# Gate and up tiles beside the last chunk's attention: three filled groups a tile in place of two, with fewer plain steps ahead of them

## The chip, the core and the metric

The kernel runs on one core of a Trainium2 chip. The metric is the device time of one execution in microseconds; of several runs the median is given. A core has TensorE (matmuls; PE in the profile, its weight loads PEld), VectorE (DVE), ScalarE (ACT), GpSimd (POOL) and SyncE (SP, which here only issues transfers). Each engine works through its own queue in order. Matmuls write to PSUM, which has eight banks of 128 x 512 fp32 here, and the other engines read the results there.

## The reference

One transformer block on 2048 rows of width 512, with 32 heads of 16 and a gated feed-forward of width 1792; the six modulation vectors come from a condition `c`.

```python
h = _layernorm(x, axis=-1) * (1 + ca) + sa
x = x + ga * _A_ref(h, A_wqkv, A_wo)          # softmax attention, then wo
h = _layernorm(x, axis=-1) * (1 + cb) + sb
x = x + gb * _B_ref(h, B_w_gate, B_w_up, B_w_down)   # (silu(x@w_gate) * (x@w_up)) @ w_down
```

## The kernel before, in words

The rows are worked on in four chunks of 512 queries. After the projections the kernel is one long attention loop: 32 units (four chunks of eight groups of four heads), each of 16 **steps**, 512 steps in all; a step is one tile of 128 keys. While the attention of one chunk runs, the output projection and the feed-forward of the chunk before are done beside it. The stretch of this change lies beside the last chunk's attention, where the feed-forward of chunk 2 (the last but one, `ci == last - 1`) is done.

A step has four **pairs** (`pair_of`, L982). A pair is one score matmul (`score`, L565: keys by queries, 50 rows of the array, 512 columns) and one matmul for the row maxima of a unit 20 steps ahead (`max_one`, L514: 48 rows). The two use opposite halves of the array's rows and run side by side. ScalarE turns the score into an exponential (L573), VectorE reduces the other one (L525); until they have read their bank, no new matmul can write it. Which banks serve is set by `bank` for scores and `four` for maxima. For the last 20 steps no maxima are left, and a pair is a score alone.

The order of the work is written out by hand, in two forms:

- `plain(steps)` (L1046) issues windows of three pairs and then some PV steps (`pv_step`, L575: exponentials by values, all 128 rows). Scores use three banks (4, 5, 6), maxima four (0, 3, 1, 2). Two PV half steps belong to each attention step; at the end of a plain stretch one more is issued, to catch up.
- `filled(places, work)` (L1061) issues eight pairs, which is two steps, with other work between them, and then the PV half steps that are due (four, once it runs). After pair r it takes `places[r]` **slots** of the work. A slot is two matmuls on opposite row halves (L789), one into each of the two banks of `FBANKS`, 3 and 6. Scores have two banks (4, 5), maxima three (0, 1, 2), bank 7 gathers the PV sums. When the maxima are over, `ALONE` replaces the places, and scores take turns over five banks.

A **gate and up tile** (`gate_up`, L854) computes 128 of the 1792 columns, gate in one bank and up in the other: 24 slots, 12 in each of two phases (`accumulate`, L778). In the second phase the two row halves trade banks. The two phases fill two groups with the places `TWO`, twelve slots each, and the PV matmuls stand between them. At the last slot ScalarE is given `th` (the tanh of the gate, L862). The rest, `q` (L866) and `m` (L868) on VectorE and the split of `m` on POOL (L870, L871), is put on the list `posts`; `hook()` (L914) issues what is on the list, at the end of each group. The tile's call also issues the next tile's 1 MB weight load on SP (`load_gu`, L713). The **down** steps (`down`, L878) have twelve slots in one group, with the places `DOWN`; their row halves trade banks too, and there a wait on ScalarE (L798) stands between the phases: it waits for the first phase's last matmuls, and the second phase's first matmul waits for it.

What belongs to a step's number (loads of the next units, the closing of a unit, the turning of the row maxima) is issued by `after(i)` from `end_steps` (L1040) and stays with that number. The row maxima of a unit are turned by `max_rows` (L527) if this falls in a plain stretch, and by `max_turned` (L545), with eight small DMAs on SP, if it falls in a filled one.

For chunk 2 the loop at L1090 issues plain steps up to step 403, four groups for the output projection, twelve plain steps for the second layer norm, then `REST` = 24 plain steps, and then the jobs: tiles 0, 1 and 2, two down steps, two tiles, two down steps, and so on up to tile 10. The nine tiles 0 to 8 take 36 steps before the change. Tile 8 ends where the maxima do.

Of the kernel before, what the change touches and what calls it, by code (L numbers as in the profile page):

```python
# [45 lines left out]
PTS = 13  # L46
FBANKS = (3, 6)
KEEP = 7
REST = 24
NORM = 9  # L50
STARTS = (147, 275, 403)
TWO = (0, 3, 2, 2, 2, 2, 1, 0)
DOWN = (0, 3, 3, 0, 3, 3, 0, 0)
ALONE = {TWO: (0, 4, 0, 4, 0, 4, 0, 0), DOWN: (0, 6, 0, 0, 0, 6, 0, 0)}


def run(it):
    for _ in it:
        pass


def take(it, k):
    run(islice(it, k))
# [40 lines left out]
def block_kernel(ctx, tc, x, wqkv, wo, w_gate, w_up, w_down, c, w_mod, out):  # L104
# [393 lines left out]
    last = NC - 1  # L498
# [132 lines left out]
    def tile_mid():  # L631
        return pf.tile([P, 2, CW], F32R, name="mid", tag="mid", bufs=3)

    def tmp(name):
        return pf.tile([P, CW], F32, name=name, tag="tmp", bufs=4)
# [142 lines left out]
    def accumulate(outs, lhs, rhs, nk, after, halves, by_k=False, trade=False):  # L778
        ends = []


        terms = [(k, a, b) for k in range(nk) for a, b in ((0, 0), (0, 1), (1, 0))]
        z = len(terms) - 1
        if halves:
            for ph in range(2):
                for j, (k, a, b) in enumerate(terms):
                    for e in (ph, 1 - ph):
                        rows = slice(64 * (ph ^ e), 64 * (ph ^ e) + 64)
                        mm = nc.tensor.matmul(outs[e], lhs(e, a, k)[rows], rhs(b, k)[rows],  # L789
                                              start=(ph == 0 and j == 0), stop=(j == z and (ph == 1 or trade)),  # L790
                                              skip_group_check=(ph == 1 and trade))
                        if trade and j == z * (1 - ph):
                            if ph == 0:
                                ends.append(mm.ins.name)
                            else:
                                tc.add_manual_dep(mm.ins, seen.ins.name, SYNC, reason="row halves trade banks")
                    if trade and j == z and ph == 0:
                        seen = nc.scalar.nop()  # L798
                        for name in ends:
                            tc.add_manual_dep(seen.ins, name, SYNC, reason="row halves trade banks")  # L800
                    if j == z and ph:
                        after()
                    yield
        else:
            order = [(e, j) for e in range(2) for j in range(z + 1)]
            for e, j in sorted(order, key=lambda o: o[1] // 3) if by_k else order:
                k, a, b = terms[j]
                nc.tensor.matmul(outs[e], lhs(e, a, k), rhs(b, k), start=(j == 0), stop=(j == z))  # L808
                if e == 1 and j == z:
                    after()  # L810
                yield
# [31 lines left out]
    def out_pair(ch, t0, outs, halves):  # L843
        return accumulate(outs, lambda e, a, k: ch.oT[a][:, k, (t0 + e) * P:(t0 + e + 1) * P],
                          lambda b, k: ch.wo[k // 2][:, b, k % 2, :], NK,
                          lambda: posts.append(lambda: add_o(ch, t0, outs, True)), halves)
# [4 lines left out]
                nc.tensor.matmul(pt, ch.oT[a][:, k, t * P:(t + 1) * P], ch.wo[k // 2][:, b, k % 2, :],  # L851
                                 start=(k == 0 and a == b == 0), stop=(k == NK - 1 and a == 1))

    def gate_up(ch, f, outs, halves):  # L854
        ch.load_gu(f + ch.ahead)
        if f == 0:
            ch.load_wd(0)
        ch.mid[f] = mid = tile_mid()

        def after():  # L860
            th = tmp("th")
            nc.scalar.activation(th, outs[0], AF.Tanh, scale=0.5)  # L862

            def later():
                q = tmp("q")
                nc.vector.scalar_tensor_tensor(q, th, 1.0, outs[0], op0=ALU.add, op1=ALU.mult)  # L866
                m32 = tmp("m32")
                nc.vector.tensor_mul(m32, outs[1], q)  # L868
                slow = halves or (ch.ci, f) == (last - 1, NF - 2)
                (nc.gpsimd.tensor_copy if slow else nc.scalar.copy)(mid[:, 0, :], m32)  # L870
                (nc.gpsimd if slow else nc.vector).tensor_sub(mid[:, 1, :], m32, mid[:, 0, :].bitcast(F32))  # L871
            posts.append(later)

        w = ch.w.pop(f)
        return accumulate(outs, lambda e, a, k: w[:, 2 * e + a, k, :], lambda b, k: ch.hT[b][:, k, :], NK, after,
                          halves)

    def down(ch, m, t0, outs, halves):  # L878
        def later():
# [27 lines left out]
    def scaled(ch):  # L907
        ch.load_gu(0)
        ch.norm_scale(nc.gpsimd)
        ch.nt = [tile_mid().bitcast(F32) for _ in range(2)]  # L910
        for t in range(4):
            ch.normalize(t)

    def hook():  # L914
        while posts:
            posts.pop(0)()
# [61 lines left out]
    halves = [(i, half) for i in range(n) for half in range(2)]  # L978
# [3 lines left out]
    def pair_of():  # L982
        nonlocal done
        i = done // 4 - 1
        most = 4 * n - 4 * (LEAD - 1)
        h = (ORDER if done < most else (0, 1, 2, 3))[done % 4]
        work = [lambda: score(i + 1, h)]
        if done < most:
            work.insert(1 - h % 2, lambda: max_one(done + 4 * (LEAD - 1)))
        for f in work:  # L990
            f()
        done += 1
        if side:
            side.pop(0)()

    for i in range(-LEAD, -1):
# [7 lines left out]
        if i == -2:  # L1004
            four, work = three, bank
# [11 lines left out]
    def pvs(most, by_halves):  # L1017

        nonlocal owed
        if by_halves:  # L1020
            most, owed = most + owed, 0
        while most and halves and 4 * halves[0][0] + 8 <= done:
            i, half = halves.pop(0)
            pv_step(i, half)
            most -= 1
            if i % 16 == 15 and half:
                close_unit(i // 16, done // 4 - 1)
                if by_halves:
                    break
        if by_halves and most and halves and 4 * halves[0][0] + 8 <= done:  # L1030
            owed = most

    def turns_behind():
        for b in list(behind):
            b[0] -= 1
            if not b[0]:
                b[1]()
                behind.remove(b)

    def end_steps():  # L1040
        nonlocal ended
        while ended < done // 4:
            after(ended - 1)
            ended += 1

    def plain(steps, tails=()):  # L1046

        nonlocal four, bank, beside
        beside = False
        assert steps % WIN == 0 and done % 4 == 0  # L1050
        four, bank = Turn(0, 3, 1, 2), Turn(4, 5, 6)
        for w in range(4 * steps // WIN):
            for _ in range(WIN):
                pair_of()
            if w < len(tails) and tails[w]:
                tails[w](four())
            pvs((HALVES[(w - 2) % 4] if done > 8 else 0) + (w == 4 * steps // WIN - 1), True)
            turns_behind()
            end_steps()

    def filled(places, work):  # L1061

        nonlocal four, bank, beside
        beside = True
        four, bank = three, Turn(4, 5)
        if done >= 4 * n - 4 * (LEAD - 1):
            places, bank = ALONE.get(places, places), Turn(4, 5, 0, 1, 2)
        for r in range(len(places)):
            pair_of()
            take(work, places[r])  # L1070
            if r % 4 == 3:
                end_steps()
        hook()
        pvs(6, False)
        turns_behind()
# [12 lines left out]
    outs = [banks[b] for b in FBANKS]  # L1088
    pvs(3, False)
    for ci in range(last):  # L1090
        plain(STARTS[ci] - done // 4)
        ch = chunks[ci]
        for t0 in (0, 2):
            work = out_pair(ch, t0, outs, True)
            filled(TWO, work)
            filled(TWO, work)
        behind.append([4, lambda: scaled(ch)])
        tails = [lambda tp, k=k: ch.turned(tp, k) for k in range(NK)]
        plain(NORM, [None] * NORM + tails[:3])
        plain(WIN, tails[3:])  # L1100
        if ci == last - 1:
            plain(REST)
        for _ in range(len(ch.jobs) - (KEEP if ci == last - 1 else 0)):
            job, args = ch.jobs.pop(0)
            if args == (NF // FG - 1, 0):
                plain(WIN)
            work = job(ch, *args, outs, True)
            for places in (TWO, TWO) if job is gate_up else (DOWN,):
                filled(places, work)
    chunks[last - 1].load_gu(NF - 2)  # L1110
    filled((0,) * 4, iter(()))

# [22 lines left out]
    ch, chp = chunks[last], chunks[last - 1]  # L1135
# [54 lines left out]
```

## Time and profile before

| | us |
|---|---|
| median of 3 runs (lowest to highest) | 1827.27 (1826.89 to 1827.74) |
| the profiled execution's own time | 1826.86 |
| its span, first to last instruction | 1825.0 |

The profile is of one execution. The page's first part gives each engine's busy time; its fourth part follows the chain of work that ended last, back from the end. Windows cut the span into stretches, the view in order of time lists single instructions. A matmul's row starts when it starts; its end is modelled, so matmuls that follow each other overlap in the rows (0.39 us long, one every 0.23 us). "L571 PE" is the score's matmul, "L571 PEld" the load of its weights. An arrow behind an idle time names what ended it. Lines are those of the kernel before. In all views of one execution times count from the span's start.

### The profile page before, as it was taken

What the parts mean: (1) busy time and instruction counts of PE and PEld (TensorE: products, weight loads), DVE (VectorE), ACT (ScalarE), POOL (GpSimd) and SP (SyncE); (2) the same over time, 40 slices, a digit from 0 to 9 for tenths busy, and PEclk for the clock granted to TensorE, in tenths of its full rate; (3) what the DMA queues carried; (4) which work ended last, traced back from release to release, by engine and by line L of the source; (5) the groups of instructions that cost most, each with busy time, mean ns of one, the idle gap of its engine ahead of it and who ended that gap; (6) DMA issues with size and microseconds to landing.
All of it is one profiled execution on the core that took longest, in us unless ns stands there. A gap on an engine that the chain in (4) does not pass through costs nothing.

```text
span 1825.0 us, 40961 instructions
## 1 busy us (share of the span) xinstructions
PE 1816.3 (100%) x16904; PEld 1202.5 (66%) x16904; DVE 1521.2 (83%) x2554; ACT 1248.0 (68%) x2358; POOL 459.9 (25%) x538
## 2 busy tenths in 40 slices
PE   9999999999999999999999999999999999999999
PEld 7876444444465777776565777776564577777887
DVE  5578999999999888888999888889999988832544
ACT  4223888888888766777888767767888876673211
POOL 3612544556223111111123111111113011131200
PEclk9999999999999999999999999999999999999999
DMA  9883876667845444453544554444643536333742
GB/s 307 288 232 138 203 199 172 179 167 199 207 81 125 103 122 143 115 149 70 145 110 105 141 125 118 122 118 91 161 80 57 116 90 157 134 123 120 279 167 108
DMA packets 80486, 267.62 MB, mean 147 GB/s; under 512 B 19604, under 2 KB 24212, under 8 KB 59620
## 3 DMA queue, kind: packets, MB, share of 16 engines
q1 hardware_dynamic: 61324, 179.71, 34.0%
q0 software_dynamic: 18288, 84.49, 19.5%
q8 instruction: 133, 2.18, 0.5%
q10 hardware_dynamic: 688, 0.80, 0.1%
q14 instruction: 53, 0.43, 0.1%
HBM read 201.85 MB, written 62.13 MB: 145 GB/s over the span
## 4 chain that ended last, share of the span: by engine, by line
PE 83%; DVE 14%; ACT 1%; DMA 0%; issue 0%; SPq 0%; DVEq 0%
PE bank L586 21%; PE bank L789 20%; PE bank L571 14%; DVE mx L525 14%; PE bank L523 11%; PE bank L808 8%; PE bank L213 7%; PE bank L851 1%; PE bank L772 0%; DMA wm_ab<-in_w_mod 0%; PE bank L165 0%; ACT sq L832 0%; DVE v_flat L882 0%; PE bank L537 0%; SPq L261 0%
## 5 line engine op out<-in xcount | busy, mean ns | idle before, releaser
L525 DVE TENSOR_REDUCE mx<-bank 128x1 f32<-128x512 f32 x2048 | 1273.3, 681 | 111.0 <-PE bank L523 63.7
L571 PE MATMUL bank<-qop,kop 50*128 50x512 f32 x2048 | 729.7, 426 | 0.4 <-ACT pt__16494 L573 0.2
L523 PE MATMUL bank<-kop,qop 48*128 48x512 f32 x2048 | 724.6, 425 | 0.3
L571 PEld LDWEIGHTS bank<-qop,kop 50*128 50x128 f32 x2048 | 343.1, 184 | 168.9 <-issue 49.8
L523 PEld LDWEIGHTS bank<-kop,qop 48*128 48x128 f32 x2048 | 342.8, 184 | 106.2 <-DVE mx L525 62.1
L789 PE MATMUL bank<-act,wgu 64*128 64x512 f32 x1872 | 303.5, 392 | 0.0
L789 PEld LDWEIGHTS bank<-act,wgu 64*128 64x128 f32 x1872 | 199.4, 187 | 22.5
L613 POOL TENSOR_TENSOR on<-o,rb 128x512 f32<-128x512 f32 x31 | 39.9, 1286 | 507.8 <-DMA rb<-d_dr 359.0
L789 PE MATMUL bank<-wd,mid 64*128 64x512 f32 x912 | 131.6, 391 | 0.0
L870 POOL CAST mid<-m 128x512 fp32r<-128x512 f32 x40 | 24.4, 609 | 380.5 <-DVE m L868 273.7
L789 PEld LDWEIGHTS bank<-wd,mid 64*128 64x128 f32 x912 | 92.2, 186 | 11.2
L213 PE MATMUL bank<-hT,wqs 128*128 128x512 f32 x384 | 94.4, 397 | 0.4 <-DVE wqs L353 0.4
L866 DVE SCALAR_TENSOR_TENSOR q<-th,bank 128x512 f32<-128x512 f32 x56 | 38.3, 683 | 54.2 <-ACT th L862 54.2
L213 PEld LDWEIGHTS bank<-hT,wqs 128*128 128x128 f32 x384 | 70.6, 188 | 19.1 <-issue 3.2
L862 ACT ACTIVATE th<-bank 128x512 f32<-128x512 f32 x56 | 33.2, 594 | 57.9 <-PE bank L808 57.9
L882 DVE TENSOR_TENSOR x<-bank,x 128x512 f32<-128x512 f32 x84 | 53.9, 685 | 16.1 <-PE bank L789 16.1
L868 DVE TENSOR_TENSOR m<-bank,q 128x512 f32<-128x512 f32 x56 | 38.7, 692 | 21.7 <-PE bank L808 19.7
L871 POOL TENSOR_TENSOR mid<-m,mid 128x512 fp32r<-128x512 f32 x40 | 51.7, 1292 | 3.3
L808 PE MATMUL bank<-wd,mid 128*128 128x512 f32 x216 | 51.3, 393 | 0.0
L213 PE MATMUL bank<-wqs,hT 128*128 128x512 f32 x192 | 48.0, 398 | 0.0
L789 PE MATMUL bank<-wgu,act 64*128 64x512 f32 x288 | 47.6, 392 | 0.0
L808 PEld LDWEIGHTS bank<-wd,mid 128*128 128x128 f32 x216 | 40.4, 188 | 8.9
(6300 smaller groups left out, 5137.3 us busy)
## 6 DMA issues: line engine op xcount, KB each, us to landing
wgu<-gu_dr SPq DMA_DIRECT2D x48, 1024.0 KB
wd<-wd_dr SPq DMA_DIRECT2D x28, 1024.0 KB
kop<-kd SPq DMA_DIRECT2D x33, 768.0 KB
kop<-kd POOLq DMA_DIRECT2D x29, 768.0 KB, 8.8
gu_dr<-wgu POOLq DMA_DIRECT2D x14, 1024.0 KB, 13.6
kd<-prt SPq DMA_DIRECT2D x16, 512.0 KB
qd<-prt SPq DMA_DIRECT2D x16, 512.0 KB
kop<-gu_dr SPq DMA_DIRECT2D x8, 1024.0 KB
```

The costliest lines, as they stand in the source:

```text
L213: nc.tensor.matmul(pt, lhs(a, k), rhs(b, k), start=(n == 0), stop=(n == 3 * nk - 1))
L523: nc.tensor.matmul(pm, qop[u][rows, s, qt * P:(qt + 1) * P], kop[u % 3][rows, s, kc * CW:(kc + 1) * CW], start=True, stop=True)
L525: nc.vector.tensor_reduce(mx[u][:, b, s, qt, kc:kc + 1], pm, op=ALU.max, axis=AX.X)
L571: nc.tensor.matmul(sp, kop[u % 3][rows, h // 2, kt * P:(kt + 1) * P], qop[u][rows, h // 2, :], start=True, stop=True)
L586: nc.tensor.matmul(pv[u][32 * h:32 * h + 32, cols], v_flat[:, e0:e0 + 32], p_[h][:, cols], start=(kt == 0 and half == 0), stop=(kt == 15), ...
L613: mul.tensor_mul(on, o, rb)
L789: mm = nc.tensor.matmul(outs[e], lhs(e, a, k)[rows], rhs(b, k)[rows], start=(ph == 0 and j == 0), stop=(j == z and (ph == 1 or trade)), sk ...
L808: nc.tensor.matmul(outs[e], lhs(e, a, k), rhs(b, k), start=(j == 0), stop=(j == z))
L866: nc.vector.scalar_tensor_tensor(q, th, 1.0, outs[0], op0=ALU.add, op1=ALU.mult)
L868: nc.vector.tensor_mul(m32, outs[1], q)
L871: (nc.gpsimd if slow else nc.vector).tensor_sub(mid[:, 1, :], m32, mid[:, 0, :].bitcast(F32))
L882: nc.vector.tensor_add(ch.x2[:, t, :], outs[e], ch.x2[:, t, :])
```

## The change

Tiles 0 to 8 of chunk 2 (`SPREAD` = 9) are spread over three filled groups in place of two, with 9, 8 and 7 slots (`THREE`). Each tile thus takes six steps, two more than before, and `REST` falls from 24 plain steps to 6, so that the number of steps is the same. The first phase now ends inside the second group, after its first three slots; so these tiles get the wait of the down steps between their phases (`trade`). With `soon`, `hook()` is called after each pair too, so `q`, `m` and the split are issued right after the last slot's pair (pair 5 of the third group) and no longer at the group's end. The third group of tile 8 lies where no maxima are left and has places of its own in `ALONE`.

```diff
-REST = 24
+REST = 6
...
-ALONE = {TWO: (0, 4, 0, 4, 0, 4, 0, 0), DOWN: (0, 6, 0, 0, 0, 6, 0, 0)}
+THREE = ((0, 2, 2, 1, 2, 1, 1, 0), (0, 3, 0, 2, 1, 1, 1, 0), (0, 2, 2, 1, 1, 1, 0, 0))
+SPREAD = 9
+ALONE = {THREE[2]: (0, 4, 0, 3, 0, 0, 0, 0), TWO: (0, 4, 0, 4, 0, 4, 0, 0), DOWN: (0, 6, 0, 0, 0, 6, 0, 0)}
...
-    def gate_up(ch, f, outs, halves):
+    def gate_up(ch, f, outs, halves, trade=False):
...
         return accumulate(outs, lambda e, a, k: w[:, 2 * e + a, k, :], lambda b, k: ch.hT[b][:, k, :], NK, after,
-                          halves)
+                          halves, trade=trade)
...
-    def filled(places, work):
+    def filled(places, work, soon=False):
...
             take(work, places[r])
+            if soon:
+                hook()
             if r % 4 == 3:
                 end_steps()
...
-            work = job(ch, *args, outs, True)
-            for places in (TWO, TWO) if job is gate_up else (DOWN,):
-                filled(places, work)
+            spread = job is gate_up and ci == last - 1 and args[0] < SPREAD
+            work = job(ch, *args, outs, True, *((True,) if spread else ()))
+            for places in THREE if spread else (TWO, TWO) if job is gate_up else (DOWN,):
+                filled(places, work, spread)
```

## Rows read from the trace of the kernel before

**Rows 1.** The page: busy time by engine; the chain that ended last, by engine.

```profile
PE 1816.3 (100%) x16904; PEld 1202.5 (66%) x16904; DVE 1521.2 (83%) x2554; ACT 1248.0 (68%) x2358; POOL 459.9 (25%) x538
...
PE 83%; DVE 14%; ACT 1%; DMA 0%; issue 0%; SPq 0%; DVEq 0%
```

**Rows 2.** Windows, score matmuls alone (L571, PE): stretch, its us, busy (count), clock.

```profile
1393.47:1452.40 58.93, 33.11 (x96) 1.00 0.31 57
1408.02:1444.11 36.09, 20.42 (x60) 1.00 0.43 71
...
1506.80:1533.95 27.15, 12.56 (x32) 1.00 0.79 185
...
1601.76:1608.32 6.56, 3.26 (x8) 1.00 0.47 176
1608.32:1614.14 5.82, 1.70 (x9) 1.00 0.03 5
```

**Rows 3.** Windows, all engines: plain stretch, one tile; PE, PEld, DVE, ACT, POOL.

```profile
1393.47:1452.40 58.93, 58.80 (x592) 28.58 (x588) 58.22 (x101) 50.88 (x102) 4.91 (x6) 1.00 0.31 57
1466.07:1479.61 13.54, 13.54 (x148) 10.55 (x144) 11.66 (x19) 9.62 (x17) 1.91 (x2) 1.00 0.57 125
```

**Rows 4.** Groups by line, plain stretch 1408.02 to 1444.11: busy, mean ns | idle before.

```profile
L525 DVE TENSOR_REDUCE mx<-bank 128x1 f32<-128x512 f32 x62 | 37.2, 674 | 0.0
```

**Rows 5.** Order of time, one filled group with twelve slots: start, length, instruction.

```profile
1527.18 0.50 PE L571 MATMUL bank<-qop,kop 50*128 50x512 f32 x1
...
1527.52 0.39 PE L571 MATMUL bank<-qop,kop 50*128 50x512 f32 x1
...
1528.36 0.18 PEld L571 LDWEIGHTS bank<-qop,kop 50*128 50x128 f32 x1
...
1529.17 0.40 PE L571 MATMUL bank<-qop,kop 50*128 50x512 f32 x1
...
1529.88 0.39 PE L571 MATMUL bank<-qop,kop 50*128 50x512 f32 x1
...
1531.74 0.41 PE L571 MATMUL bank<-qop,kop 50*128 50x512 f32 x1
...
1533.95 0.49 PE L571 MATMUL bank<-qop,kop 50*128 50x512 f32 x1
```

**Rows 6.** Order of time, the same group: ScalarE and VectorE.

```profile
1527.71 0.60 ACT L573 ACTIVATE pt__18965<-bank 128x512 f32<-128x512 f32 x1 [1.67 <-PE bank L523]
1528.21 0.59 ACT L573 ACTIVATE pt__18970<-bank 128x512 f32<-128x512 f32 x1
...
1529.63 0.60 ACT L573 ACTIVATE pt__18992<-bank 128x512 f32<-128x512 f32 x1
1530.31 0.60 ACT L573 ACTIVATE pt__18999<-bank 128x512 f32<-128x512 f32 x1
...
1532.91 0.68 DVE L866 SCALAR_TENSOR_TENSOR q<-th,bank 128x512 f32<-128x512 f32 x1
1533.62 0.69 DVE L868 TENSOR_TENSOR m<-bank,q 128x512 f32<-128x512 f32 x1
```

**Rows 7.** Order of time, p2 of the group at 1513.56, after a late exponential.

```profile
1514.82 0.40 PE L523 MATMUL bank<-kop,qop 48*128 48x512 f32 x1
1514.83 0.18 PEld L571 LDWEIGHTS bank<-qop,kop 50*128 50x128 f32 x1
1514.83 0.49 PE L571 MATMUL bank<-qop,kop 50*128 50x512 f32 x1
```

**Rows 8.** Line L571, 1452.40 to 1608.32: idle before it until (us, times).

```profile
  ACT pt__19691 L573: 0.2, 1
```

**Rows 9.** Line L798, the wait between phases: count, ns min/median/max.

```profile
L798 ACTq EVENT_SEMAPHORE  x38: 17/17/17, 630.2 to 1656.6; - x38
```

**Rows 10.** Order of time, filled groups: SP and POOL.

```profile
1500.66 4.38 SPq L562 DMA_DIRECT2D qop<-turned  x8
...
1521.44 1.29 POOL L871 TENSOR_TENSOR mid<-m,mid 128x512 fp32r<-128x512 f32 x1
```

## The prediction

> **What bounds the kernel now.** I read the page first: TensorE counts as busy for the whole span, and the chain that ended last lies on it for 83% [rows 1]. Its busy time is modelled, so this alone does not say that it is full. Next I cut the stretch beside the last chunk's attention into windows and counted its score matmuls, four to a step [rows 2]. The 24 plain steps ahead of the tiles take 58.93 us; 15 of them, clear of both ends, take 36.09 us, or 2.406 us a step. Four filled groups of two steps, which are two gate and up tiles, take 27.15 us: 6.79 us a group, 13.58 us a tile. The two kinds have different limits. In the plain stretch VectorE is busy for 58.22 of 58.93 us [rows 3], and its maxima follow each other with no idle time [rows 4], 60 of them in the 36.09 us, 0.60 us each. In a filled tile VectorE has work for 11.66 and ScalarE for 9.62 of 13.54 us [rows 3]; TensorE sets the pace. So the idea of the change has a ground in the rows: TensorE has room in plain steps, VectorE in filled ones.
>
> The third view is one filled group in order of time [rows 5] with its exponentials [rows 6]. I call its eight pairs p0 to p7. From p1 (1527.52) to p7 (1531.74) there are six pairs and twelve slots, 18 units in 4.22 us: **0.234 us a unit**. From p7 to the next p0 (1533.95), with the PV matmuls between, it is **2.21 us**. The number that decides is in the same rows: how long a score bank is taken. p4's score starts at 1529.88 and its exponential at 1530.31, 0.43 later; p3's takes 0.46; I use 0.44. An exponential lasts 0.60. p0's ends at 1528.31, and the weight load of p2's score, which writes the same bank, starts at 1528.36, 0.05 later. If that load had to wait, the matmul behind it is shown with 0.49 us in place of 0.39, as at 1514.83 [rows 7]: its weights were not there early, 0.10 more. A bank thus comes round in 0.44 + 0.60 + 0.05 + 0.10 = **1.19 us**. Filled groups have two score banks, so pair r+2 can follow pair r by 1.19 us at the soonest. Two pairs and three slots last 5 x 0.234 = 1.17 us, which just covers it; the old places keep three or more slots between any such two pairs inside a group. Even so the load idles 0.2 us for an exponential in some groups (eight such lines, one shown) [rows 8].
>
> **The change part by part.** *Removed:* 18 plain steps at 2.406, 43.3 us, or 4.81 a tile. The catch-up at the end of the plain stretch stays, with the six steps that stay. A tile may therefore grow from 13.58 to **18.39 us** before anything is lost: 6.13 a group.
>
> *Spread:* matmuls, exponentials, maxima and PV steps are the same in number; only where they stand changes. With two slots between pair r and r+2, four units are 0.94 us and the pair is 0.25 late; with one slot 0.49. I walk one group each, from p0's row at 0. From the rows, p0's exponential runs from 0.53 to 1.13, p1 stands at 0.34, its exponential follows the first by 0.50 and ends at 1.63. So p2 stands at 1.28 at the soonest, p3 at 1.78; these include the 0.15 of release and weight load.
> Nine slots: p2 1.28 (1.04 by slots), p3 1.98, p4 2.47, p5 3.17, p6 3.67, p7 4.36 (4.14 by slots; p5's exponential ends at 4.21). With 2.21: 6.57.
> Eight slots: p2 1.28, p3 1.78 (1.51 by slots), p4 2.48, p5 2.97, p6 3.67, p7 4.17. With 2.21: 6.38.
> Seven slots: p2 1.28, p3 1.98, p4 2.47, p5 3.17, p6 3.67, p7 4.36 (3.90 by slots). With 2.21: 6.57.
> The tile: **19.52 us**, 1.13 over the 18.39. Eight tiles: 9.0 us. A group with no slot at all would still need p3 at 1.78, p5 at 2.97 and p7 at 4.16, so 6.37: no placing of 24 slots in three such groups gets under 19.11.
>
> *The ninth tile* ends where the maxima are over and five banks take the scores. Its third group has seven slots: the old twelve-slot group there takes 5.82 [rows 2], less 5 x 0.234 is 4.65. So 6.57 + 6.38 + 4.65 = 17.60 against 6.56 + 5.82 [rows 2] + 4.81 = 17.19: 0.4 us more.
>
> *The traded banks:* one ScalarE wait a tile, 17 ns [rows 9], behind p1's exponential in the eight-slot group. Queued behind it are p2's exponential and later ones, and TensorE's thirteenth slot waits for it. The twelfth slot is through at about 1.5 on the same scale, before p1's exponential ends, and the thirteenth comes after p3 at 1.78 or later. I cost it at nothing; without that cover it is at most the 0.05 of a release.
>
> *The earlier hook:* q and m (0.68 and 0.69 [rows 6]) stand on VectorE's queue behind p5's maximum, where they wait for th, which stands behind p5's exponential: th would run from 4.11 to 4.70, q and m to about 6.1. Behind them are the maxima of p6 and p7, done at about 6.8 and 7.4. The next group's p1 is at 6.91 and needs the bank of p6's maximum: just in time. VectorE's spare time over a tile covers it: 24 maxima at 0.60 and 1.37 make 15.8 of 19.5. If the cover is gone it is some 0.1 us a tile; I put 0 in the sum and 0.9 in the upper end.
>
> *Moved queues:* each tile's 1 MB weight load on SP is issued one tile ahead and gets 6 us more. The row turn of one more unit falls in a filled group, with eight small DMAs, 4.38 us on SP [rows 10], ahead of such a load; that load has a tile's time. POOL's cast and subtraction (1.29 us for the latter [rows 10]) feed a down step at least one tile later. Nothing on the path.
>
> **Sum:** 9.0 + 0.4 = +9.4 us on the profiled execution's 1826.86, 1836.3; the median shown, 1827.27, stands 0.4 above it. I take **1836.5 us**. Lower bound of the cost: if the 0.10 of the late weight load does not count (the pair's other half of the rows goes on meanwhile [rows 7]), a bank comes round in 1.09, and the same walk gives p7 at 4.14, 3.97 and 4.06, groups of 6.35, 6.18 and 6.27, a tile of 18.80: +3.3 us over eight tiles, nothing on the ninth, 1830.2. I take the upper one because [rows 7] shows the longer matmul in this very place. Upper bound: 0.1 more in each of 27 groups (units that close, late maxima), 1839.2.
>
> **Rivals.** *TensorE alone counts* (faster). If waits for banks vanish in the freedom of the two row halves, a tile costs its units: 3 x 6.79 less 12 x 0.234 = 17.55, 0.84 under 18.39; the ninth 6.09 + 5.85 + 4.65 = 16.59, 0.6 under. That is -7.3 us: **1819.6**. It decides for this side if p7 comes 3.92 us after p0 on average or sooner; against it stands that an exponential cannot start before its score, and that [rows 8] show the wait already at three slots. The Trainium skill (Perfetto Trace Analysis, Optimization Strategy) says that where the most contended engine changes over time, interleaving the regimes may help; by that rule the time is this rival's. The same section says that a repeated gap on the engine that should be full can mean too little SBUF or PSUM for the next tile; the load waits of [rows 8] agree with that.
> *Half of it is absorbed* (no change): a tile of 18.2 to 18.8 with the low price of the release: 1824 to 1830.5.
> *VectorE becomes the bound:* if the late q and m reach the next group's maxima each time and its own waits add to that, some 0.5 us a group after the seven-slot one, +4 us on top: **1840.5**.
>
> **Chances.** About 0.2%, 3.7 us, is what a measurement of this kernel can tell from no change. Slower as forecast, VectorE's rival with it: 0.76. Half absorbed: 0.09. TensorE alone: 0.15. Range 1826 to 1842: it takes in the lower price, the upper bound and VectorE's rival, and leaves out the faster one. The forecast's own range is 1830 to 1840.
>
> **What would show it.** Right: three groups of 6.4 to 6.6 us in place of two of 6.79; idle time of the score's weight load ended by exponentials at p2 and p7 of each group; the plain stretch down to about 15.6 us; fewer score matmuls of 0.39 us. Wrong: groups of 6.1, 5.9 and 5.6 us with no such idle time (TensorE alone), or idle time ended by maxima (VectorE).

## The result, and the profile after

The changed kernel takes **1837.2 us** (median of 6 runs, 1835.9 to 1839.9); the kernel before 1827.58 (6 runs, 1826.89 to 1830.2). The ratio is 1.005, with an interval of 1.0037 to 1.0063: half a per cent slower. The profiled execution took 1837.56 us, with a span of 1835.7; that of before had 1825.0. TensorE's granted clock is 1.00 in all stretches below. In the kernel after, every line from the one that held the score has a number two higher: the score is L573, its exponential L575, the matmul of a maximum L525 and its reduction L527, `th` L864, `q` L868.

First the page of the kernel after, its busy times and its chain, which answer to [rows 1]:

```profile
PE 1825.8 (99%) x16898; PEld 1202.4 (65%) x16898; DVE 1518.9 (83%) x2556; ACT 1247.2 (68%) x2357; POOL 459.2 (25%) x538
...
PE 95%; DVE 2%; ACT 1%; DMA 0%; SPq 0%; issue 0%; DVEq 0%
```

TensorE counts as busy for 9.5 us more, though it has no more work; the other engines have what they had. The chain must not be read as a measure here: VectorE's share of it falls from 14% of the span to 2%, some 220 us, while the change shortens the plain stretch by 44 us. In experiments below that hardly differ from this kernel it is 8% and 14%. I read this as one other branch taken far back, where TensorE and VectorE are both near their limits; no run separates it. What the change did is in the windows.

Windows of the kernel after, score matmuls alone (L573, PE): stretch, its us, busy (count), clock, DMA share, GB/s. They are the plain stretch; the first group of tile 0; tile 3 whole; the three groups of tile 4; tile 8 whole, and its third group.

```profile
1394.34:1409.33 14.99, 8.59 (x24) 1.00 0.41 128
1409.33:1416.71 7.38, 3.41 (x8) 1.00 0.25 102
1482.37:1501.82 19.45, 10.35 (x25) 1.00 0.52 141
1501.82:1508.36 6.54, 3.41 (x9) 1.00 0.67 192
1508.36:1514.69 6.33, 3.45 (x9) 1.00 0.11 41
1514.69:1521.23 6.54, 3.51 (x8) 1.00 0.03 5
1606.97:1624.57 17.60, 8.58 (x24) 1.00 0.58 207
1619.86:1624.57 4.71, 1.60 (x8) 1.00 0.02 3
```

Groups of nine, eight and seven slots take 6.54, 6.33 and 6.54 us, those of twelve slots took 6.79 [rows 2]. They repeat within 0.03 us from tile 1 to tile 7. A tile takes 19.45 us in place of 13.58; the break-even was 18.39.

Tile 3 again, all engines (PE, PEld, DVE, ACT, POOL), answers to the second line of [rows 3]:

```profile
1482.37:1501.82 19.45, 19.45 (x197) 12.33 (x194) 15.60 (x27) 13.66 (x25) 0.28 (x1) 1.00 0.52 141
```

VectorE has 15.60 of 19.45 us and ScalarE 13.66. PE counts as busy throughout, because a matmul's modelled time fills small gaps: waits of some 0.2 us between matmuls don't show in this column. They show in the weight loads, which are next.

The group of seven slots at 1514.69, in order of time: weight loads of scores, from p0 to p7 (in brackets the idle time of the weight loads and what ended it), then the score matmuls, up to the next p0, and some exponentials.

```profile
1514.68 0.18 PEld L573 LDWEIGHTS bank<-qop,kop 50*128 50x128 f32 x1 [0.41 <-issue]
...
1515.87 0.18 PEld L573 LDWEIGHTS bank<-qop,kop 50*128 50x128 f32 x1 [0.19 <-ACT pt__18743 L575]
...
1517.05 0.18 PEld L573 LDWEIGHTS bank<-qop,kop 50*128 50x128 f32 x1 [0.19 <-ACT pt__18767 L575]
1517.76 0.18 PEld L573 LDWEIGHTS bank<-qop,kop 50*128 50x128 f32 x1 [0.40 <-ACT pt__18776 L575]
...
1518.94 0.18 PEld L573 LDWEIGHTS bank<-qop,kop 50*128 50x128 f32 x1 [0.36 <-ACT pt__18788 L575]
```

```profile
1514.69 0.50 PE L573 MATMUL bank<-qop,kop 50*128 50x512 f32 x1
1515.03 0.39 PE L573 MATMUL bank<-qop,kop 50*128 50x512 f32 x1
1515.87 0.50 PE L573 MATMUL bank<-qop,kop 50*128 50x512 f32 x1
...
1518.33 0.41 PE L573 MATMUL bank<-qop,kop 50*128 50x512 f32 x1
1518.94 0.50 PE L573 MATMUL bank<-qop,kop 50*128 50x512 f32 x1
1521.23 0.49 PE L573 MATMUL bank<-qop,kop 50*128 50x512 f32 x1
```

```profile
1515.22 0.60 ACT L575 ACTIVATE pt__18743<-bank 128x512 f32<-128x512 f32 x1 [1.70 <-PE bank L573]
1515.72 0.59 ACT L575 ACTIVATE pt__18756<-bank 128x512 f32<-128x512 f32 x1
...
1518.29 0.60 ACT L575 ACTIVATE pt__18788<-bank 128x512 f32<-128x512 f32 x1
```

Read them together. p0's exponential ends at 1515.22 + 0.60 = 1515.82; the load for p2, which writes the same bank, starts 0.05 later, and the matmul behind it lasts 0.50 in place of 0.39. p5's exponential ends at 1518.89, and p7's load starts at 1518.94, again 0.05 later. Four of the six loads that reuse a bank, those of p2, p4, p5 and p7, waited for an exponential. p7 comes 4.25 us after p0. In the old twelve-slot group it took 4.56, with five slots more, which are 1.17 us of TensorE's time [rows 5]: spreading the work gave back 0.31 of them.

**Where the time went.** I cut both traces at the start of the plain stretch and at the end of tile 8. The tiles lie between groups of down steps, which are counted apart.

| | before, us | after, us | difference |
|---|---|---|---|
| plain stretch | 58.93 | 14.99 | -43.94 |
| tiles 0 to 7 | 108.54 | 156.49 | +47.95 |
| tile 8 | 12.38 | 17.60 | +5.22 |
| six groups of down steps | 40.82 | 41.15 | +0.33 |
| the stretch | 220.67 | 230.23 | +9.56 |

The rest of the span's 10.7 us is 0.87 ahead of the stretch, where the code is the same (profiles of other versions with the same code ahead start the stretch between 1392.36 and 1394.23), and 0.27 behind it.

### The profile page after: what moved, and what is told of

The parts are those of the page before. It is cut to its first block, busy times and chain, and to the rows that moved or that the text cites. A ratio compares the mean times of both kernels' runs of the same rounds, so it can differ in the third digit from the quotient of the medians.

```text
span 1835.7 us, 40976 instructions
## 1 busy us (share of the span) xinstructions
PE 1825.8 (99%) x16898; PEld 1202.4 (65%) x16898; DVE 1518.9 (83%) x2556; ACT 1247.2 (68%) x2357; POOL 459.2 (25%) x538
## 4 chain that ended last, share of the span: by engine, by line
PE 95%; DVE 2%; ACT 1%; DMA 0%; SPq 0%; issue 0%; DVEq 0%
PE bank L588 26%; PE bank L791 20%; PE bank L573 18%; PE bank L525 15%; PE bank L810 8%; PE bank L215 7%; DVE mx L527 2%; PE bank L853 1%; PE bank L774 0%; DMA wm_ab<-in_w_mod 0%; PE bank L167 0%; ACT sq L834 0%; PE bank L539 0%; DVE v_flat L884 0%; PE bank L538 0%
## 5 line engine op out<-in xcount | busy, mean ns | idle before, releaser
L527 DVE TENSOR_REDUCE mx<-bank 128x1 f32<-128x512 f32 x2048 | 1271.5, 690 | 121.1 <-PE bank L525 76.2
L573 PE MATMUL bank<-qop,kop 50*128 50x512 f32 x2048 | 742.4, 429 | 1.3 <-ACT pt__3913 L575 0.6
L525 PE MATMUL bank<-kop,qop 48*128 48x512 f32 x2048 | 727.7, 425 | 0.3
L573 PEld LDWEIGHTS bank<-qop,kop 50*128 50x128 f32 x2048 | 344.1, 184 | 189.4 <-issue 53.1
L525 PEld LDWEIGHTS bank<-kop,qop 48*128 48x128 f32 x2048 | 344.0, 184 | 101.2 <-DVE mx L527 57.6
L791 PE MATMUL bank<-act,wgu 64*128 64x512 f32 x1872 | 318.0, 393 | 0.0
L791 PEld LDWEIGHTS bank<-wd,mid 64*128 64x128 f32 x912 | 92.9, 186 | 10.7
L868 DVE SCALAR_TENSOR_TENSOR q<-th,bank 128x512 f32<-128x512 f32 x56 | 38.3, 684 | 56.2 <-ACT th L864 56.2
L864 ACT ACTIVATE th<-bank 128x512 f32<-128x512 f32 x56 | 33.2, 594 | 57.9 <-PE bank L810 57.9
```

What stands on the lines that cost most here:

```text
L525: nc.tensor.matmul(pm, qop[u][rows, s, qt * P:(qt + 1) * P], kop[u % 3][rows, s, kc * CW:(kc + 1) * CW], start=True, stop=True)
L527: nc.vector.tensor_reduce(mx[u][:, b, s, qt, kc:kc + 1], pm, op=ALU.max, axis=AX.X)
L573: nc.tensor.matmul(sp, kop[u % 3][rows, h // 2, kt * P:(kt + 1) * P], qop[u][rows, h // 2, :], start=True, stop=True)
```

## The experiments

My theory was the prediction's: two score banks, each of which comes round in 1.19 us, hold a spread group at about 6.35 us, whatever the number of its slots. The rivals were VectorE (its queue, made worse by the early `q` and `m`), the traded halves, ScalarE's exponentials as such, and a plain lack of TensorE time. Nine kernels ran; each ratio is to runs of the kernel before on the same chip.

### The hook at the end of the group again

```diff
-                filled(places, work, spread)
+                filled(places, work)
```

> The changed kernel with the hook at the end of each group again, so that q and m stand behind the maxima of the third group's last pairs, as before the change. Theory (waits for the two score banks): nothing changes, groups of 6.55, 6.35 and 6.55 us, total within 1 us of the changed kernel's 1837. Rival (the early q and m hold up VectorE and with it TensorE): the group after the seven-slot one gets shorter by 0.1 to 0.5 us, total 1833 to 1836.

Measured: 1838.88 us (1838.04 to 1839.86), ratio 1.0064 [1.0049 to 1.0079]. The seven-slot group, whose end the edit changes (windows of this kernel, score matmuls):

```profile
1514.47:1521.02 6.55, 3.50 (x9) 1.00 0.03 5
```

It is 6.54 in the kernel after. Tiles are 19.40 to 19.46. The total is 1.7 us over the changed kernel's, more than I expected, but it lies outside the tiles, and the intervals overlap. The early hook neither costs nor gains anything in the tiles.

### Other places, floor unchanged

```diff
-THREE = ((0, 2, 2, 1, 2, 1, 1, 0), (0, 3, 0, 2, 1, 1, 1, 0), (0, 2, 2, 1, 1, 1, 0, 0))
+THREE = ((0, 3, 1, 2, 1, 1, 1, 0), (0, 3, 0, 2, 1, 1, 1, 0), (0, 3, 0, 2, 1, 1, 0, 0))
```

> The changed kernel with the same 9, 8 and 7 slots at places that fit the banks' rhythm: (0,3,1,2,1,1,1,0), (0,3,0,2,1,1,1,0), (0,3,0,2,1,1,0,0). Theory (two score banks, 1.19 us round trip): by the same walk p7 stands at 4.17 in all three, so three groups of 6.33 to 6.38 us whatever their slots, a tile of 19.0 to 19.1 in place of 19.45, total 3 to 4 us under the changed kernel and still about 6 us over the kernel before. Rival (a fixed cost for each group more, wherever its slots stand): 19.4 to 19.5 as now, total 1837. Rival (TensorE's own work): 6.1, 5.9 and 5.6 us.

Measured: 1834.05 us (1833.37 to 1836.84), ratio 1.0039 [1.0024 to 1.0053]. Windows of this kernel, score matmuls, groups of nine, eight and seven slots:

```profile
1499.32:1505.72 6.40, 3.33 (x8) 1.00 0.73 204
1505.72:1512.06 6.34, 3.45 (x8) 1.00 0.11 44
1512.06:1518.41 6.35, 3.53 (x9) 1.00 0.03 5
```

The three groups now cost the same within 0.06 us, though they hold nine, eight and seven slots; two slots are 0.47 us of TensorE's time. So TensorE's work doesn't set the length of a group here. Places that put three slots ahead of p2, and none or one between p2 and p3, bring 3 us of the 10 back and no more. All three lie within 0.03 us of the prediction's floor of 6.37 a group; the nine-slot one is 0.02 over the range that was written down for this run.

### A third bank for scores, taken from the maxima

```diff
-    three = Turn(0, 1, 2)
+    three, two = Turn(0, 1, 2), Turn(0, 1)
...
-        four, bank = three, Turn(4, 5)
+        four, bank = (two, Turn(4, 5, 2)) if soon else (three, Turn(4, 5))
```

> The changed kernel with bank 2 given to the scores in the spread tiles: three score banks (4, 5, 2), two banks (0, 1) for the maxima. Theory (a pair waits for the bank of the pair two before it): the exponential no longer holds the score, but the maximum holds its bank for 0.44 + 0.69 + 0.05 + 0.10 = 1.28 us, so the waits move to VectorE and grow: groups of about 6.9, 6.8 and 6.9 us, with up to 0.5 more in the group after q and m, a tile of 20.6 to 21.0, total 1846 to 1850; the idle time of weight loads is ended by maxima. Rival (ScalarE's exponentials as such are the limit): shorter, since a score no longer waits for the one two before it, under 19 us a tile.

Measured: 1847.17 us (1846.45 to 1849.03), ratio 1.011 [1.0095 to 1.0125]; tiles of 20.58 to 20.87 us. Windows of one tile's eight-slot group, score matmuls; then, in order of time, weight loads of maxima (L525) in it:

```profile
1512.37:1519.30 6.93, 3.49 (x9) 1.00 0.10 38
```

```profile
1513.68 0.18 PEld L525 LDWEIGHTS bank<-kop,qop 48*128 48x128 f32 x1 [0.32 <-DVE mx L527]
...
1516.40 0.18 PEld L525 LDWEIGHTS bank<-kop,qop 48*128 48x128 f32 x1 [0.56 <-DVE mx L527]
```

The wait changes sides: loads for the maxima wait for reductions, which last 0.69 us against 0.60 for an exponential, and two banks hold them harder. All eight banks of PSUM are in use, and with whole maxima to reduce, none of the three can be taken from them.

### The two-slot groups back, trade and early hook alone

```diff
-REST = 6
+REST = 24
...
-            for places in THREE if spread else (TWO, TWO) if job is gate_up else (DOWN,):
+            for places in (TWO, TWO) if job is gate_up else (DOWN,):
```

> The traded banks and the early hook alone: nine tiles in two groups of twelve slots with 24 plain steps ahead, as before the change, but with the wait between the phases and the hook after each pair. Theory: both cost next to nothing, a tile of 13.6 to 13.7, total within 1 us of the kernel before. Rival (the wait or the hook makes the loss): 14.5 us a tile, total 1832 to 1837.

Measured: 1827.61 us (10 runs, 1826.39 to 1829.68), ratio 1.0004 [0.9995 to 1.0014]: the kernel before. Windows, score matmuls, plain stretch and one tile:

```profile
1393.05:1451.98 58.93, 33.12 (x96) 1.00 0.29 58
1519.99:1533.50 13.51, 6.24 (x16) 1.00 0.54 121
```

In groups of twelve slots the trade's wait on ScalarE and the early hook cost nothing. The whole loss comes with the spreading.

### Full rows, and third banks on top of them

To free a bank for scores without touching the maxima, the slots of these tiles were made one matmul over all 128 rows, gate first and then up, so that bank 6 lies idle while gate is summed. Three kernels: the full rows alone; bank 6 as a third score bank in the nine-slot group; and, besides, bank 3 as one in the seven-slot group, with `q` taken early so that it is free, and other places.

```diff
...
-                          halves, trade=trade)
+                          halves and not trade)
...
```

> The changed kernel with another order in the nine spread tiles: each slot is one matmul over all 128 rows, first the twelve of the gate into bank 3, then the twelve of up into bank 6, so no banks are traded. Places, score banks and everything else stay. It is the control for the next run. Theory (two score banks): the waits stay, groups of 6.5 to 6.65, 6.35 to 6.45 and 6.5 to 6.65 us, a tile of 19.4 to 19.7, total 1836 to 1840. Rival (the traded halves make the loss): 18.4 or less.

```diff
...
-        four, bank = three, Turn(4, 5)
+        four, bank = three, Turn(4, 5, *more)
...
-                filled(places, work, spread)
+                filled(places, work, spread, FBANKS[1:] if places is THREE[0] else ())
```

> The run before, and in the nine-slot group of each tile bank 6, which up does not use yet, serves as a third score bank (4, 5, 6). Theory: there a pair waits for the exponential three pairs before it, which 1.19 us of round trip leave no wait for; that group falls to 6.07 to 6.2 us (units 6.09, or the maxima after q and m), the other two stay, a tile is 0.35 to 0.45 shorter, total 3 to 4 us under the run before. Rival (ScalarE or the group itself sets the length): the nine-slot group stays at 6.5.

```diff
-THREE = ((0, 2, 2, 1, 2, 1, 1, 0), (0, 3, 0, 2, 1, 1, 1, 0), (0, 2, 2, 1, 1, 1, 0, 0))
+THREE = ((0, 2, 1, 2, 1, 2, 1, 0), (0, 3, 0, 2, 1, 1, 1, 0), (0, 2, 1, 2, 1, 1, 0, 0))
...
+                filled(places, work, spread, FBANKS[1:] if places is THREE[0] else FBANKS[:1] if places is THREE[2] else ())
```

> The run before, with th taken right after the gate's last slot and q at the end of the second group, so that bank 3 is free in the third group and serves its scores there (4, 5, 3); places (0,2,1,2,1,2,1,0), (0,3,0,2,1,1,1,0), (0,2,1,2,1,1,0,0). Theory: only the eight-slot group keeps its 6.34; the nine-slot one takes about 6.07, the seven-slot one 6.0 to 6.1, where the maxima with three banks set a floor (p7 at 3.84, 6.05 in all), a tile of 18.4 to 18.6, total 1826.5 to 1830: the loss is gone and there is no gain over the kernel before. Rival (TensorE alone counts once banks are there): 6.1, 6.0 and 5.6, 17.7 a tile, total 1821.

Measured: 1875.17 (ratio 1.0263 [1.0249 to 1.0277]), 1875.54 (1.0266 [1.0252 to 1.028]) and 1873.56 us (1.0255 [1.0241 to 1.0269]). All three miss every number that was written down, and by the first of them one sees why. Its nine-slot group (window, score matmuls), and a piece of the same tile's seven-slot group in order of time:

```profile
1517.48:1525.95 8.47, 3.71 (x8) 1.00 0.60 172
```

```profile
1536.15 0.50 PE L573 MATMUL bank<-qop,kop 50*128 50x512 f32 x1
1536.57 0.19 PEld L810 LDWEIGHTS bank<-act,wgu 128*128 128x128 f32 x1 [0.25 <-issue]
1536.57 0.51 PE L810 MATMUL bank<-act,wgu 128*128 128x512 f32 x1
...
1537.01 0.18 PEld L573 LDWEIGHTS bank<-qop,kop 50*128 50x128 f32 x1 [0.25 <-issue]
...
1537.01 0.49 PE L573 MATMUL bank<-qop,kop 50*128 50x512 f32 x1
```

A full-row slot between two half-row pairs starts 0.42 us after the first, and the next pair 0.44 after it, where two units were 0.234 apart. At each such change the weight load starts only when the matmul behind it does, and that matmul is a long one. It is the change that costs, not the full-row matmul: in the kernel before, thirteen of them in a row take 3.23 us (L808, from 1700.30), 0.24 from one to the next. A tile grows to some 23.9 us, and the third bank shortens nothing: with it the same nine-slot group takes 8.47 us again. These runs say nothing on what a third bank does for the half-row form: inconclusive.

### Short maxima: VectorE's work cut, banks as they are

```diff
...
-        nc.vector.tensor_reduce(mx[u][:, b, s, qt, kc:kc + 1], pm, op=ALU.max, axis=AX.X)
+        nc.vector.tensor_reduce(mx[u][:, b, s, qt, kc:kc + 1], pm[:, 0:64] if short else pm, op=ALU.max, axis=AX.X)
...
-        nc.scalar.activation(p_, sp, AF.Exp, scale=SCALE)
+        nc.scalar.activation(p_, sp, AF.Exp, scale=SCALE / 16 if u >= NU - 4 else SCALE)
...
```

> The changed kernel with VectorE's work in the spread tiles cut: a maximum reads 64 of its 512 columns, about 0.22 us in place of 0.69 (the other columns are left out, and the exponentials of the last units are taken at a sixteenth of the scale, so that they stay finite). Matmuls, places and banks stay. Theory (the two score banks hold the pairs): nothing changes, groups of 6.55, 6.34 and 6.55 us, total 1836 to 1839. Rival (VectorE, its maxima with q and m behind them): groups of 6.1, 5.9 and 5.6, total 1820 to 1825.

Measured: 1837.63 us (1836.44 to 1839.25), ratio 1.0059 [1.0042 to 1.0076]. Windows of the three groups, all engines (PE, PEld, DVE, ACT, POOL):

```profile
1500.83:1507.39 6.56, 6.56 (x71) 4.29 (x68) 1.80 (x8) 4.47 (x8) 3.51 (x4) 1.00 0.62 179
1507.39:1513.74 6.35, 6.35 (x69) 4.09 (x65) 2.31 (x11) 4.44 (x9) 0.00 (x0) 1.00 0.11 42
1513.74:1520.28 6.54, 6.54 (x66) 3.87 (x62) 2.99 (x10) 4.83 (x9) 0.27 (x1) 1.00 0.02 5
```

VectorE's work falls from 15.6 to 7.1 us a tile, and the groups stay at 6.56, 6.35 and 6.54. VectorE does not set their length.

### Short maxima, and three score banks

The edit above, and that of the bank taken from the maxima: with short reductions two banks are nearly enough for them.

```diff
...
-        four, bank = three, Turn(4, 5)
+        four, bank = (two, Turn(4, 5, 2)) if soon else (three, Turn(4, 5))
...
```

> The run before, and bank 2, which the short maxima can spare, goes to the scores: three score banks (4, 5, 2), two for the maxima (0, 1), which come round in 0.44 + 0.22 + 0.15 = 0.81 us. Theory: the waits for a score bank are gone and TensorE's units are left, groups of 6.1, 5.85 and 5.6 to 5.7 us, a tile of 17.5 to 17.7, total 1819 to 1822, some 16 us under the run before. Rival (a cost of every filled group, or ScalarE's exponentials as such): the groups stay over 6.3, total 1834 to 1838.

Measured: **1823.19 us** (8 runs, 1821.59 to 1824.89), ratio 0.9976 [0.9965 to 0.9986]: 14.4 us under the run before it, from which only the banks set it apart, three for scores and two for maxima. Windows of three groups, all engines; then, in order of time, weight loads of p2 and p7 (p7's maximum, L527, too) and the score matmul of p7 in the seven-slot one (the score is L575 in this kernel):

```profile
1495.35:1501.62 6.27, 6.27 (x70) 4.75 (x66) 2.13 (x11) 4.41 (x8) 3.19 (x3) 1.00 0.71 208
1501.62:1507.42 5.80, 5.80 (x68) 3.96 (x65) 2.31 (x11) 4.23 (x9) 0.60 (x1) 1.00 0.12 45
1507.42:1513.12 5.70, 5.70 (x66) 3.82 (x63) 2.65 (x9) 4.66 (x9) 0.00 (x0) 1.00 0.03 6
```

```profile
1508.27 0.18 PEld L575 LDWEIGHTS bank<-qop,kop 50*128 50x128 f32 x1
...
1510.82 0.18 PEld L527 LDWEIGHTS bank<-kop,qop 48*128 48x128 f32 x1 [0.28 <-DVE mx L529]
1510.83 0.18 PEld L575 LDWEIGHTS bank<-qop,kop 50*128 50x128 f32 x1
...
1510.83 0.50 PE L575 MATMUL bank<-qop,kop 50*128 50x512 f32 x1
```

The idle time ended by exponentials is gone from p2, p4, p5 and p7. p7 comes 1510.83 - 1507.42 = 3.41 us after p0, where it took 4.25. Groups have again about the length of their slots: 5.80 with eight and 5.70 with seven, where units give 5.85 and 5.62. What is left at p7 of the seven-slot group is a wait for a maximum's bank, and the score's load stands behind it. The nine-slot groups of tiles 1 to 7 take 6.06 to 6.40, where units give 6.09. In the longest, that of tile 1 at 1427.83, the load of p0's maximum starts 0.35 us after that of p0's score: it waits for a reduction of the group before, which stands on VectorE's queue behind `q` and `m`, and `q` had waited for `th` (7.6 us over eight tiles). In order of time:

```profile
1426.49 0.69 DVE L870 SCALAR_TENSOR_TENSOR q<-th,bank 128x512 f32<-128x512 f32 x1 [1.01 <-ACT th L866]
...
1427.92 0.35 DVE L529 TENSOR_REDUCE mx<-bank 128x1 f32<-128x64 f32 x2
```

```profile
1428.18 0.18 PEld L527 LDWEIGHTS bank<-kop,qop 48*128 48x128 f32 x1 [0.17 <-DVE mx L529]
```

A tile is 17.58 to 17.94 us (tiles 1 to 7), on the gaining side of 18.39. The median is 1.2 us over the range that was written down. The rivals of this run, a cost of every filled group and ScalarE's exponentials as such, wanted groups over 6.3; those of eight and seven slots are far under it.

## Why the prediction was right

**The forecast and its sign.** 1836.5 us was written down and 1837.2 came, in the range, on the side that had the chance of 0.76. The reason written down, the round trip of a score bank, is the one that the runs bear out: cutting VectorE's work in half changes nothing, the late hook changes no group of the tiles, trade and early hook without the spreading cost nothing, and with the short maxima a third score bank gives 14.4 us. The trade was not taken out of the spread form by itself, but it stays in the run with the third score bank, whose eight- and seven-slot groups are within 0.1 us of their units.

**The round trip.** 1.19 us was put together from rows of before. The rows of after show 0.53 to p0's exponential, 0.60, 0.05, and a load that starts with its matmul (0.50 long). p2 is shown 1.18 after p0, where the walk had 1.28, because the walk booked the 0.10 of the longer matmul at its start; with 0.10 added it is 1.28, and p7 4.25 + 0.10 = 4.35 against 4.36. The lower price, which would have left the 0.10 out, gave groups of 6.35, 6.18 and 6.27; 6.54, 6.33 and 6.54 were measured. Choosing the upper one was right, though [rows 7] alone didn't settle it. By the trace of before, thirteen loads between 1452.40 and 1608.32 waited for an exponential, and eleven of them still started 0.03 to 0.11 us ahead of their matmul, which lasted 0.40 to 0.47; the one shown in [rows 8] is of this kind, in a group of down steps. In the spread groups the load mostly starts with its matmul.

**The groups.** 6.57, 6.38 and 6.57 were forecast: 0.03 to 0.05 too much in each. Tiles 1 to 7 are 19.44 in the mean (the tiles' 174.09 less 20.40 and 17.60, by 7) against 19.52, which makes 0.56 us too much over seven. Tile 8 was forecast at 17.60 and took it, by luck: its groups took 6.55, 6.34 and 4.71 where 6.57, 6.38 and 4.65 were forecast. What would show the mechanism was forecast as idle time at p2 and p7; it stands at p4 and p5 as well. The walk has these two at the bank's time too (2.47 and 3.17), but I had not named them.

**The row turns.** The turn that was forecast to move into a filled group did so, in tile 2, and "nothing on the path" was right for it: its eight transfers (SP, kernel after) start in a group that takes 6.35 us, and the next takes 6.56.

```profile
1461.79 4.39 SPq L564 DMA_DIRECT2D qop<-turned  x8
```

What the forecast did not see is another turn, one in the plain form (`max_rows`). It begins at the end of the plain stretch and its matmuls are issued two windows or groups later; with six plain steps this is behind tile 0's first group, which takes 7.38 in place of 6.54 us. In order of time, kernel after, TensorE (small matmuls of the turn, then the next p0):

```profile
1415.76 0.27 PE L537 MATMUL bank<-minus,m 128*16 128x128 f32 x1
...
1415.98 0.38 PE L539 MATMUL bank<-minus,nm 128*16 128x128 f32 x2
1416.71 0.50 PE L573 MATMUL bank<-qop,kop 50*128 50x512 f32 x1 [0.35 <-ACT mr L541]
```

The turn's matmuls write the score bank that is next in turn, and p0 waits until ScalarE's copy of the turned maxima (L541) has read it. The plain stretch, forecast at 15.6 us, is 14.99; it held two such turns before and ends none now, and I read the 0.6 as the price of one in its old place, which no run separates. Tile 0's 20.40 against 19.52, less 0.6, leaves +0.28.

**What was left out.** Six down groups are 0.05 us longer each (41.15 against 40.82); no run tells why. By the sum +9.4 us was expected in the stretch and +9.56 measured: tiles 1 to 7 are 0.56 under, turn and plain stretch 0.28 over, the down groups 0.33 over, and the eight tiles of before took 108.54 where 8 x 13.58 is 108.64, 0.10 over. The agreement to 0.2 is thus partly luck: small errors of both signs, among them a turn that the forecast had not seen.

**The rivals.** *TensorE alone* needed p7 at 3.92 or sooner on average; it came at 4.25 in groups of nine and seven slots and at 4.05 in those of eight. Its time, 1819.6, is near what the third score bank gives: with it, and with short maxima, 1823.19 was measured, 3.6 over; some of that is that tiles took 17.58 to 17.94 and not 17.55. The Trainium skill (Perfetto Trace Analysis, Optimization Strategy) says that where the most contended engine changes over time, interleaving the regimes may help, and that a repeated gap on the engine that should be full can mean too little PSUM for the next tile. The runs agree with the second, by the 14.4 us of one score bank more. The changed kernel does not gain by the first (1837.2 against 1827.58 us); the run with the third score bank does (1823.19 against 1827.65), but its maxima leave out seven eighths of their columns. *VectorE the bound* (1840.5) fell with the short maxima. *Half absorbed* fell with the groups of 6.54.

No version here beats the kernel before with all of its work done. From the runs with bank 2 given to the scores I conclude that the spread form would need a third score bank beside three for whole maxima; no run shows it, and scores, maxima, gate, up and PV already hold all eight. Fewer slots a group can't help, since the floor of 6.34 doesn't sink with them (the run with other places); by the units, groups of ten slots would take 6.32 (6.79 less 2 x 0.234, an estimate), close to it, but I have not tried them.

## What to carry to other kernels

Before work is spread over more rounds of a loop, work out how soon a round may follow another: the time from the write of a buffer to its release, over the number of buffers. Below that floor, filler work is cover and not cost, and taking it away frees nothing. Price the spread form at the larger of floor and work, per round, and compare it with what a plain round costs; an engine that seems to have room in the sum of a stretch may have none at that rhythm.

## What the runs showed of the hardware

Changing between half-row pairs of matmuls and full-row ones cost about 0.2 us each way (0.42 and 0.44 us between starts, against 0.234 between units of the same kind): with 24 full-row slots strewn among pairs, a tile grew from 19.45 to 23.9 us though it held 24 matmuls fewer. I had expected the full-row slots to cost about what the paired ones did.

And a wait for a bank can cost up to 0.10 us more than itself. In the kernel after, where the weight load that waited starts together with its matmul, the matmul lasts 0.50 us in place of 0.39, and its exponential starts 0.53 after it in place of 0.44 (p5 above: 1517.76 and 1518.29). It is the late load that costs, not the bank: p0 of each group, whose load waits for no exponential, shows the 0.50 too. And not every load that waits is late. One of the kernel before, in a group of down steps, is shown first, then its matmul, 0.11 later and short:

```profile
1503.31 0.18 PEld L571 LDWEIGHTS bank<-qop,kop 50*128 50x128 f32 x1 [0.16 <-ACT pt__18647 L573]
```

```profile
1503.42 0.40 PE L571 MATMUL bank<-qop,kop 50*128 50x512 f32 x1
```
